# Regrouping TensorE's small-tile products in a planned attention, mixture-of-experts and channel-mix kernel

## The chip, the cores and the metric

The kernel runs on one core of one Trainium2 chip. The metric is the device time of one execution in microseconds (us). Three runs of the kernel before took 386.15, 383.17 and 384.91 us; the median is 384.91 us.

## The reference, cut to what matters

Three stages follow each other, all in float32. Two sequences of 768 tokens are processed.

```python
# stage 1: 8 heads of 64, a local window of 16 plus 24 block summaries
k_sum = k.reshape(B, H, nb, block, D).max(axis=3)
v_sum = v.reshape(B, H, nb, block, D).mean(axis=3)
scores_all = concat([where(|i - j| < 16, q @ k.T / 8, -1e9), q @ k_sum.T / 8 + log(32)])
x = softmax(scores_all) @ concat([v, v_sum])
...
# stage 2: 4 experts, each a causal attention of its own (Hd = 64); the best 2 per token are summed
for e in range(E):
    a = softmax(causal((x @ wq[e]) @ (x @ wk[e]).T / 8))
    ye = a @ (x @ wv[e]) @ wo[e]
    out += (e in topk) * w_e * ye
...
# stage 3: channel mix
k = maximum(xk @ w_k, 0); v = (k * k) @ w_v; r = sigmoid(xr @ w_r); return r * v
```

`xk` and `xr` are mixes of each token with the one before it.

## The kernel before, in words

Stage 1 goes over 12 tiles of 128 tokens (six per sequence). For a tile, `stage1_scores` makes the scores of 4 head pairs (L585: products of 64 rows by 64 columns, a quarter of TensorE's array each); VectorE (DVE) adds the mask and takes the maximum (L599), ScalarE (ACT) the exponential (L602), the rows are normalized (L610, on GpSimd (POOL), DVE or ACT); `stage1_trans` turns the weights with TensorE (PE, L637: full array) into PSUM, and ACT or DVE copies them out (L368, L369); `stage1_out` multiplies them with the values (L655: half of the array per product), and ACT and DVE copy the result from the one bank "a1" into `x` as a high and a low part (L368, L376). The means of the values per block (`val_sums0`, L516) are products with a matrix of ones kept in `cst`; they need all value tiles of the first sequence, and ACT, DVE and POOL then copy them into 12 value tiles (`put_val_sums`, L368, L369, L371) before a tile's L655.

Stage 2 goes over 4 chunks of 384 tokens: projections (`proj_all`, L734, L771), scores of each expert (L846, L847; DVE L855, ACT L865), and for each pair of experts `attend`: the weights are cut into 128x128 blocks, three blocks make a block group, each group is turned for both experts (L906: full array), evicted by ACT or DVE into a buffer `th`, and multiplied with the values into the bank "a2" (L926: half of the array per product). A chunk of the first half of a sequence has 2 groups per expert pair, one of the second half 5. L937 multiplies the sum with the gate, L960 is the output projection.

Stage 3: `rec` (L1068), `hid` (L1090) and `vout` (L1113) per chunk, all on the full array. Its weights are converted by DVE and ACT first (L1003 to L1012).

Nothing runs in the order in which it is written. Every piece is recorded as an operation with a cost; `Plan.run` then places operations one at a time on the engine that is free first, by its own clock and by priorities (`BIAS` per stream), and the program is emitted in that order. Each engine works strictly in the emitted order. For PE the planner adds `tail` (47 to 52 ns) when the next operation is of another stream. A recorded operation is never interrupted by another one, but between two operations the planner may put anything. Before, the scores of a tile are 4 operations, and each run of blocks of L926 one operation, recorded one block group behind the transposes. Six PSUM banks "ps" are shared by all; buffers are given out in turn from numbered slots (`th` 4).

## Time and profile before

| | us |
|---|---|
| median of three runs | 384.91 |
| the profiled execution, its own time | 389.32 |
| span of its instructions in the profile | 387.5 |
| PE busy in the span | 363.2 |
| DVE busy | 274.3 |
| ACT busy | 230.4 |
| POOL busy | 78.9 |
| stage 3's last part on PE, from the first L1113 on | 145.4 |

How to read it: the profiled execution took 389.32 us as a whole; the profile's rows count from its first instruction and reach over 387.5 us, so 1.8 us lie around them. A row of a timeline gives start, duration, engine, line and the tiles; rows of one kind that follow each other are merged (x16), and in brackets stands how long the engine stood still before and what ended it. PE's matrix products are pipelined: the duration of a row reaches past the start of the next, so the price of a product is read from start to start. Float32 products are recorded once per pass, so a row's count is that of passes. Granted clock 1.00 is 2.4 GHz, 0.50 is 1.2 GHz.

### The profile page before, as it was taken

What the parts mean: (1) busy time and instruction counts of PE and PEld (TensorE: products, weight loads), DVE (VectorE), ACT (ScalarE), POOL (GpSimd) and SP (SyncE); (2) the same over time, 40 slices, a digit from 0 to 9 for tenths busy, and PEclk for the clock granted to TensorE, in tenths of its full rate; (3) what the DMA queues carried; (4) which work ended last, traced back from release to release, by engine and by line L of the source; (5) the groups of instructions that cost most, each with busy time, mean ns of one, the idle gap of its engine ahead of it and who ended that gap; (6) DMA issues with size and microseconds to landing.
All of it is one profiled execution on the core that took longest, in us unless ns stands there. A gap on an engine that the chain in (4) does not pass through costs nothing.

```text
span 387.5 us, 7433 instructions
## 1 busy us (share of the span) xinstructions
PE 363.2 (94%) x2704; PEld 304.9 (79%) x2704; DVE 274.3 (71%) x828; ACT 230.4 (59%) x631; POOL 78.9 (20%) x116
## 2 busy tenths in 40 slices
PE   1785999899999999999999999999999999999996
PEld 0554789767768789897787699888988899889986
DVE  2869699899999899797999999913870196202511
ACT  2967786989877886688678976404550256014500
POOL 5204601344431201150353143200010001000000
PEclk9997699999999999999999999999999999999999
DMA  8993445846041142100131530010001000100001
GB/s 273 234 287 113 137 151 162 209 146 188 26 151 57 28 143 62 43 2 0 56 108 44 176 108 2 27 54 2 0 2 54 27 3 0 47 36 1 2 27 54
DMA packets 18596, 31.41 MB, mean 81 GB/s; under 512 B 1792, under 2 KB 8960, under 8 KB 18560
## 3 DMA queue, kind: packets, MB, share of 16 engines
q1 hardware_dynamic: 18560, 30.94, 26.3%
q8 instruction: 21, 0.34, 0.4%
q14 instruction: 15, 0.12, 0.1%
HBM read 27.79 MB, written 3.15 MB: 80 GB/s over the span
## 4 chain that ended last, share of the span: by engine, by line
PE 81%; DVE 9%; DMA 7%; ACT 2%; issue 1%; SPq 0%; DVEq 0%; ACTq 0%
PE ps L1090 18%; PE ps L1113 17%; PE ps L1068 9%; PE ps L734 6%; PE a L926 5%; PE ps L960 4%; PE ps L771 4%; PE ps L906 4%; PE ps L585 3%; PE a L655 3%; PE ps L846 3%; PE ps L637 2%; PE ps L847 2%; DMA vw<-in_vp 2%; DMA qb<-in_qT 2%; DMA stage<-in_vp 2%
## 5 line engine op out<-in xcount | busy, mean ns | idle before, releaser
L602 ACT ACTIVATE pp<-pp,nm 128x120 f32<-128x120 f32 x96 | 36.7, 384 | 7.6 <-DVE nm L599 7.3
L865 ACT ACTIVATE pq<-pq,nm 128x128 f32<-128x128 f32 (+5 forms) x48 | 31.8, 664 | 8.8 <-DVE nm L855 7.0
L1119 DVE TENSOR_TENSOR wvgl<-ps,pp 128x512 f32<-128x512 f32 (+1 forms) x13 | 8.5, 650 | 39.2 <-PE ps L1113 39.2
L368 ACT ACTIVATE pp<-ps 128x512 f32<-128x512 f32 x11 | 6.6, 597 | 49.4 <-PE ps L1068 49.4
L734 PE MATMUL ps<-x,wqkh 128*128 128x384 f32 x128 | 35.1, 355 | 0.0
L855 DVE CUSTOM_DVE_ANT_0 pq<-ps,trm 128x384 f32<-128x384 f32 (+3 forms) x64 | 30.8, 500 | 1.0 <-PE ps L847 0.5
L1096 DVE SCALAR_TENSOR_TENSOR q<-ps,q 128x384 f32<-128x384 f32 x32 | 17.5, 553 | 17.3 <-ACT q L1095 17.0
L906 PE MATMUL ps<-cst,pq 128*128 128x128 f32 x168 | 28.3, 276 | 0.1
L585 PE MATMUL ps<-kw,qb 64*64 64x120 f32 x320 | 15.6, 314 | 11.2 <-DMA qb<-in_qT 7.8
L1006 POOL TENSOR_SCALAR f<-f 128x512 f32<-128x512 f32 x11 | 17.3, 1573 | 41.0 <-ACT f L1003 31.9
L637 PE MATMUL ps<-cst,pp 128*120 128x128 f32 x96 | 19.4, 319 | 5.7 <-DVE pp L610 4.0
L599 DVE CUSTOM_DVE_ANT_0 pp<-ps,msk 128x120 f32<-128x120 f32 x96 | 21.8, 274 | 4.0 <-PE ps L585 3.9
L926 PE MATMUL a<-th,vv 128*64 128x384 f32 (+2 forms) x144 | 24.4, 435 | 0.3 <-DVE fs L937 0.3
L376 DVE TENSOR_TENSOR x<-q,x 128x384 fp32r<-128x384 f32 x23 | 12.9, 581 | 16.3 <-ACT x L368 16.1
L1095 ACT ACTIVATE q<-ps 128x384 f32<-128x384 f32 x32 | 15.7, 489 | 14.1 <-PE ps L1090 12.8
L846 PE MATMUL ps<-ks,q 128*128 128x384 f32 (+3 forms) x64 | 22.2, 352 | 1.2 <-DVE nm L855 0.6
L637 PEld LDWEIGHTS ps<-cst,pp 128*120 128x120 f32 x96 | 12.3, 154 | 13.8 <-issue 9.6
L906 PEld LDWEIGHTS ps<-cst,pq 128*128 128x128 f32 x168 | 20.2, 140 | 3.6 <-issue 0.7
L368 ACT ACTIVATE th<-ps 128x384 f32<-128x384 f32 x46 | 21.2, 487 | 2.8 <-PE ps L906 2.5
L734 PEld LDWEIGHTS ps<-x,wqkh 128*128 128x128 f32 x128 | 21.2, 189 | 1.8 <-issue 1.0
L585 PEld LDWEIGHTS ps<-kw,qb 64*64 64x64 f32 x320 | 10.3, 156 | 15.3 <-ACT kw L368 11.2
L771 PE MATMUL ps<-wvgh,x 128*128 128x260 f32 x96 | 21.9, 292 | 0.0
(231 smaller groups left out, 1050.5 us busy)
## 6 DMA issues: line engine op xcount, KB each, us to landing
stage<-in_wk SPq DMA_DIRECT2D x8, 512.0 KB, 3.5
stage<-in_wv SPq DMA_DIRECT2D x8, 512.0 KB, 3.6
qb<-in_qT SPq DMA_DIRECT2D x12, 256.0 KB, 5.3
vw<-in_vp SPq DMA_DIRECT2D x16, 192.0 KB, 3.3
out_y<-wvgl SPq DMA_DIRECT2D x11, 256.0 KB, 2.0
stage<-in_wr SPq DMA_DIRECT2D x4, 512.0 KB, 3.8
kw<-in_kS SPq DMA_DIRECT2D x6, 320.0 KB, 3.8
ks<-in_kS SPq DMA_DIRECT2D x4, 400.0 KB, 5.2
```

Source lines behind the costliest of these rows:

```text
L585: mm(ps[par].t[c, i * NK:(i + 1) * NK], q.t[r, i, c], k.t[r, i, o:o + NK], start=True, stop=True)
L602: op("act", act(NK, True) + 186, lambda i=i: nc.scalar.activation(pr.t[:, i], pr.t[:, i], AF.Exp, bias=nm.t[:, i:i + 1], scale=-1.0, accum ...
L637: lambda i=i: nc.tensor.transpose(p.t[:NK, i * P:(i + 1) * P], pr.t[:, i], ident()),
L734: mm(p.t[:, :C], a.t[:, kc, cols], x.t[:, kc, :], start=(kc == 0 and i == 0), stop=(kc == KC - 1 and i == 2))
L771: mm(p.t[:, :260], x.t[:, kc, tok], a.t[:, kc, :], start=(kc == 0 and i == 0), stop=(kc == KC - 1 and i == 2))
L846: mm(p.t[:, :z - a], q1.t[:, e, tok], ks.t[:, e, a:z], start=True, stop=False)
L865: op("act", act(nk, True) + 186, lambda pr=pr, nm=nm, nk=nk, i=e2 * TPC + tq, m=nc_: nc.scalar.activation(pr.t[:, :nk], pr.t[:, :nk], AF.E ...
L906: lambda i=i, kb=kb, pr=pr: nc.tensor.transpose(p.t[:, i * P:(i + 1) * P], pr.t[:, kb * P:(kb + 1) * P], ident()),
L926: mm(acc.t[64 * e2:64 * e2 + 64, tq0 * P:(tq0 + cnt) * P], vv.t[:, kb, e * D:(e + 1) * D], ths[e2].t[:, i0 * P:(i0 + cnt) * P], start=firs ...
L1068: mm(p.t, a.t[:, kc, tok], w[2](), start=(kc == 0 and i == 0), stop=(kc == KC - 1 and i == 2))
L1090: mm(p.t[:, :C], w[2]()[:, mo:mo + P], a.t[:, kc, :], start=(kc == 0 and i == 0), stop=(kc == KC - 1 and i == 2))
L1113: mm(p.t[:, :n], a[2]()[:, tok], w[2]()[:, col], start=(m == 0 and i == 0), stop=(m == FC - 1 and i == 2))
```

## The change

PE's array can be cut: a product of 64 by 64 uses a quarter ("quarter"), one of 128 rows by 64 columns a half ("half"), the rest the whole ("full"). The change names this mode for each PE operation and regroups the operations:

- the planner charges 150 or 190 ns whenever the next PE operation has another mode (it was 47 to 52 ns for another stream), and the costs of the small products are lowered accordingly;
- the four score operations of a tile of stage 1 become one (two for the first tile);
- the value products of `attend` are recorded in steps: both groups in one operation for a chunk of 2 groups, groups 0 and 1 and then 2, 3 and 4 for a chunk of 5; the transposes of the next group are recorded ahead of a step;
- `th` gets 6 slots instead of 4, `ksm` 1 instead of 2, and the matrix of ones moves from `cst` into a tile `own` of its own that uses a slot of `x2` (one more transfer of 368 bytes per partition; `cst` has 672 instead of 1040).

```diff
-SLOTS = dict(th=4, pt=3, pp=4, stage=2)
+SLOTS = dict(th=6, pt=3, pp=4, stage=2)
...
+    SWITCH = {(a, b): 150.0 if a == "full" else 190.0 for a in ("full", "half", "quarter") for b in (
+        "full", "half", "quarter") if a != b}
...
-                if last_pe is not None and last_pe.stream != o.stream:
-                    t = max(t, clock["pe"] + last_pe.tail)
+                if last_pe is not None and last_pe.mode != o.mode:
+                    t = max(t, clock["pe"] + self.SWITCH[last_pe.mode, o.mode])
...
-    cst = buf("cst", [P, P + 5 * NB - 4 + 16])
+    cst = buf("cst", [P, P + NB + 16])
+    own = buf("x2", [P, 4 * NB - 4])
...
-                op("pe", 300, go, r=[cst, (v, "win")] + ([(v, "sum")] if s2 == 0 else []), w=[p], stream="p1v",
-                   tail=52.0)
+                op("pe", 230, go, r=[own, (v, "win")] + ([(v, "sum")] if s2 == 0 else []), w=[p], stream="p1v",
+                   mode="quarter")
...
-                def go(i=i, ps=ps):
+            def go(lo=lo, hi=hi, ps=ps):
+                for i in range(lo, hi):
                     for s2 in range(2):
...
-                op("pe", 260, go, r=[q] + kr, w=[(p, i) for p in ps], stream="p1", claim=prs + nms, tail=52.0)
+            op("pe", 205 * (hi - lo), go, r=[q] + kr, w=[(p, i) for p in ps for i in range(lo, hi)], stream="p1",
+               claim=prs + nms, mode="quarter")
...
-            several("p1o", GROUP["p1o"], i, 4, 331, av, r=[pts[0][0], pts[1][0], vs[0], vs[1]],
-                    w=[(p, i)], tail=52.0)
+            several("p1o", GROUP["p1o"], i, 4, 234, av, r=[pts[0][0], pts[1][0], vs[0], vs[1]],
+                    w=[(p, i)], mode="half")
...
-                    op("pe", pe_f(cnt * P, 64) + 60, go, r=ths + [(vv, kb)], w=[acc], stream="p2a", tail=47.0)
-
-            prev = None
-            for gi in range(len(groups) + 1):
-                cur = [tr(gi, e2) for e2 in range(2)] if gi < len(groups) else None
-                if gi > 0:
-                    vmm(gi - 1, prev)
-                prev = cur
...
+                op("pe", sum(18.0 + 1.9 * r[6] * P for r in runs), go,
+                   r=sum((ths[gi] for gi in some), []) + [(vv, r[4]) for r in runs], w=[acc], stream="p2a", mode="half")
...
+            steps = ((0, 1), (2, 3, 4)) if len(groups) == 5 else ((0, 1),)
+            for i, some in enumerate(steps):
+                ahead = some[-1] + (i + 1 < len(steps))
+                for gi in range(len(ths), ahead + 1):
+                    ths[gi] = [tr(gi, e2) for e2 in range(2)]
+                vmm(some)
```

Since the planner's costs change, the whole order changes. Counted over PE's instructions, the mode changes 112 times in the order before and 58 times in the changed one; from the first projection (the first L734) on, 92 and 41 times, 35 of the 92 in the stretch of 86 to 126 us of the profile. The same products stand ahead of the first projection in both orders: the scores of six tiles, the value sums, 36 transposes of stage 1 and the value products of four tiles. Value products of `attend` are visited 28 times before and 12 times now, scores of stage 1 22 and 10 times.

Three places show it. The first is PE in the second chunk's `attend` (`a_316` and `a_317` are the bank of the sum, `th` the turned block groups, `pq` the weights, `pp` weights of stage 1). Before:

```order
L926 MATMUL a_316_1666<-th_1585,vv_648 64x384
L926 MATMUL a_316_1666<-th_1612,vv_648 64x384
L637 MATMUL ps_1674<-cst_84,pp_1417 120x128 x2
L906 MATMUL ps_1679<-cst_84,pq_292_1234 128x128
L906 MATMUL ps_1679<-cst_84,pq_295_1373 128x128
L906 MATMUL ps_1679<-cst_84,pq_299_1408 128x128
L906 MATMUL ps_1685<-cst_84,pq_303_1480 128x128
L906 MATMUL ps_1685<-cst_84,pq_306_1499 128x128
L906 MATMUL ps_1685<-cst_84,pq_310_1532 128x128
L926 MATMUL a_316_1666<-th_1649,vv_648 64x384
L926 MATMUL a_316_1666<-th_1658,vv_648 64x384
```

And now:

```order
L913 MATMUL ps_1616<-cst_84,pq_307_1424 128x128
L913 MATMUL ps_1616<-cst_84,pq_311_1436 128x128
L939 MATMUL a_317_1625<-th_1553,vv_640 64x384
L939 MATMUL a_317_1625<-th_1564,vv_640 64x384
L939 MATMUL a_317_1625<-th_1579,vv_640 64x384
L939 MATMUL a_317_1625<-th_1592,vv_640 64x384
L662 MATMUL a_277_1639<-pt_1539,vw_113 64x64
L662 MATMUL a_277_1639<-pt_1546,vw_113 64x64
```

Two block groups now stand together, and stage 1's value products (also half) follow them without a change of mode.

The second is PE at the scores of stage 1's sixth tile, shortly ahead of the first projection (`ps_584`, `ps_585` and `ps_583`, `ps_584` are the banks of the scores, `pp_430` and `pp_458` the weights of the tile before). Before:

```order
L637 MATMUL ps_579<-cst_84,pp_430 120x128
L585 MATMUL ps_584<-kw_144,qb_90 64x120
L585 MATMUL ps_585<-kw_144,qb_90 64x120
...
L637 MATMUL ps_579<-cst_84,pp_430 120x128
...
L655 MATMUL a_95_619<-pt_488,pq_26_74 64x64
```

And now:

```order
L644 MATMUL ps_575<-cst_84,pp_458 120x128 x4
L591 MATMUL ps_583<-kw_146,qb_94 64x120
L591 MATMUL ps_584<-kw_146,qb_94 64x120
...
L662 MATMUL a_96_613<-pt_516,pq_27_74 64x64
```

Before, two of the four transposes stand between score operations; now all four stand ahead of them.

The third is DVE where the value sums (`vs`) have become ready and are copied into the value tiles (`pp` are weights of stage 1, the ISA rows their masks). Before:

```order
L610 TENSOR_TENSOR pp_286<-pp_286,rss_217 128x480
L369 COPY vw_67<-vs_409 24x512
L369 COPY vw_105<-vs_409 24x512
L369 COPY vw_122<-vs_409 24x512
L369 COPY oh_70<-vs_409 24x512
L369 COPY ol_135<-vs_409 24x512
L605 TENSOR_REDUCE rss_217<-sms_63 128x4
```

And now:

```order
L373 COPY vw_67<-vs_370 24x512
L617 TENSOR_TENSOR pp_302<-pp_302,rss_221 128x480
L606 ISA pp_374,nm_376<-ps_372,msk_76 128x120
...
L606 ISA pp_375,nm_377<-ps_373,msk_76 128x120
...
L373 COPY oh_70<-vs_370 24x512
```

Two of the twelve copies are left on DVE and stand apart; ACT has three (one before) and POOL seven (six before).

## Rows read from the trace of the kernel before

**Rows 1.** The page's shares of the chain of work that ended last, by engine.

```profile
PE 81%; DVE 9%; DMA 7%; ACT 2%; issue 1%; SPq 0%; DVEq 0%; ACTq 0%
```

**Rows 2.** Busy time by stretch: start and end in us, length, busy us (instructions) of PE, of PE's weight loads, DVE, ACT and POOL, the granted clock, DMA share, GB/s. The first stretch is from the first L734 to the first L1113, the second from there to the end.

```profile
46.30:242.08 195.78, 192.00 (x1549) 157.98 (x1546) 181.43 (x574) 155.84 (x429) 57.02 (x76) 1.00 0.31 94
242.08:387.50 145.42, 142.44 (x709) 125.54 (x707) 62.20 (x120) 44.79 (x88) 5.74 (x6) 1.00 0.06 22
```

**Rows 3.** PE's timeline ahead of the first projection.

```profile
34.81 1.08 PE L637 MATMUL ps<-cst,pp 128*120 128x128 f32 x4 [2.86 <-DVE pp L610]
35.83 1.98 PE L655 MATMUL a<-q,vw 120*64 120x64 f32 x32
39.23 0.48 PE L655 MATMUL a<-pt,oh 120*64 120x64 f32 x4 [1.42 <-DVE x L376]
...
41.13 1.54 PE L637 MATMUL ps<-cst,pp 128*120 128x128 f32 x6
...
45.24 1.15 PE L655 MATMUL a<-pt,pq 120*64 120x64 f32 x32
46.32 0.62 PE L734 MATMUL ps<-x,wqkh 128*128 128x384 f32 x2
```

**Rows 4.** Busy time by stretch, as in rows 2, for the two microseconds in which the granted clock changes.

```profile
34.00:35.00 1.00, 0.19 (x1) 0.22 (x2) 1.00 (x4) 1.00 (x5) 0.17 (x1) 0.67 0.82 193
44.00:45.00 1.00, 1.00 (x14) 0.57 (x17) 0.02 (x1) 0.01 (x1) 0.00 (x0) 0.71 0.75 263
```

**Rows 5.** Busy time by stretch, as in rows 2, for the 40 us in which stage 1 and stage 2 run side by side.

```profile
86.00:96.00 10.00, 10.00 (x163) 8.17 (x159) 9.97 (x48) 10.00 (x39) 3.87 (x7) 1.00 0.60 186
96.00:106.00 10.00, 10.00 (x86) 7.82 (x88) 9.73 (x44) 8.85 (x28) 4.70 (x5) 1.00 0.15 39
106.00:116.00 10.00, 9.71 (x98) 6.33 (x94) 9.78 (x22) 7.43 (x19) 3.79 (x3) 1.00 0.48 147
116.00:126.00 10.00, 9.95 (x75) 8.09 (x76) 9.72 (x52) 6.87 (x21) 1.45 (x3) 1.00 0.15 55
```

**Rows 6.** PE's timeline around value products of the last chunk that stand among products of `rec`.

```profile
199.46 0.86 PE L1068 MATMUL ps<-kw,x 128*128 128x512 f32 x3
200.16 0.86 PE L1068 MATMUL ps<-vw,x 128*128 128x512 f32 x3
...
201.48 0.87 PE L926 MATMUL a<-th,vv 128*64 128x384 f32 x4
202.28 0.96 PE L1068 MATMUL ps<-vw,x 128*128 128x512 f32 x3
203.16 0.65 PE L926 MATMUL a<-th,vv 128*64 128x256 f32 x4
```

**Rows 7.** The chain of work that ended last, in order of time (start, us, what): two block groups in one visit.

```profile
177.27 1.45 PE a L926 x12
```

**Rows 8.** PE's timeline around value products of the second chunk that stand among transposes.

```profile
132.14 0.87 PE L926 MATMUL a<-th,vv 128*64 128x384 f32 x4
132.94 0.43 PE L637 MATMUL ps<-cst,pp 128*120 128x128 f32 x2
133.21 0.82 PE L906 MATMUL ps<-cst,pq 128*128 128x128 f32 x6
133.96 0.87 PE L926 MATMUL a<-th,vv 128*64 128x384 f32 x4
```

**Rows 9.** PE's timeline at scores of stage 1: two tiles' scores in one visit, and a tile's scores cut by single transposes.

```profile
67.08 1.87 PE L585 MATMUL ps<-kw,qb 64*64 64x120 f32 x64
68.89 0.44 PE L906 MATMUL ps<-cst,pq 128*128 128x128 f32 x2
...
86.96 0.82 PE L637 MATMUL ps<-cst,pp 128*120 128x128 f32 x6
...
88.28 0.32 PE L637 MATMUL ps<-cst,pp 128*120 128x128 f32 x1
88.53 0.44 PE L585 MATMUL ps<-kw,qb 64*64 64x120 f32 x8
88.90 0.33 PE L637 MATMUL ps<-cst,pp 128*120 128x128 f32 x1
...
89.52 1.15 PE L655 MATMUL a<-pt,vw 120*64 120x64 f32 x32
```

**Rows 10.** DVE's timeline: the first mask row of the third tile's scores, and the copies of the value sums.

```profile
23.82 0.28 DVE L599 CUSTOM_DVE_ANT_0 pp<-ps,msk 128x120 f32<-128x120 f32 x1 [3.02 <-PE ps L585]
...
29.11 2.38 DVE L369 COPY vw<-vs 24x512 f32<-24x512 f32 x3 [0.38 <-ACT vs L368]
31.50 0.74 DVE L369 COPY oh<-vs 24x512 f32<-24x512 f32 x1
32.25 0.74 DVE L369 COPY ol<-vs 24x512 f32<-24x512 f32 x1
```

**Rows 11.** PE's timeline: the third tile's scores, which a transpose cuts in two.

```profile
20.64 1.08 PE L585 MATMUL ps<-f,qb 64*64 64x120 f32 x16 [0.96 <-DMA qb<-in_qT]
...
22.69 1.08 PE L585 MATMUL ps<-f,qb 64*64 64x120 f32 x16
```

**Rows 12.** The transfer queue's timeline: the issue of `cst`.

```profile
3.53 0.43 SPq L359 DMA_DIRECT2D cst<-in_consts  x1
```

**Rows 13.** Instructions that write `th`: count, then ns min/median/max.

```profile
L368 ACT ACTIVATE th<-ps x46: 471/489/509, 82.4 to 219.5; 128x384 f32<-128x384 f32 x46
```

More of the change, by code (lines that the diff above doesn't have):

```diff
@@ L76 @@
     __slots__ = ("ways", "eng", "cost", "fn", "preds", "succs", "bufs", "prio", "start", "end", "need", "seq", "late",
-                 "est", "prev", "stream", "tail", "lock")
+                 "est", "prev", "stream", "mode", "lock")
 class Plan:
@@ L109, in buf, with op @@
         return b
-    def op(self, eng, cost, fn, r=(), w=(), stream=None, late=0.0, bias=0.0, claim=(), ways=(), tail=0.0, lock=False):
+    def op(self, eng, cost, fn, r=(), w=(), stream=None, late=0.0, bias=0.0, claim=(), ways=(), mode="full", lock=False):
         o = Op()
@@ L115, in op @@
         o.eng, o.cost, o.fn, o.seq, o.late = eng, cost, fn, len(self.ops), late
-        o.prev, o.stream, o.tail = None, stream, tail
+        o.prev, o.stream, o.mode = None, stream, mode
         if stream:
@@ L329, in attn_moe_rwkv @@
     consts: bass.AP,
+    owns: bass.AP,
     out: bass.AP,
@@ L395, in attn_moe_rwkv, with several @@
     held = {}
-    def several(stream, size, i, n, cost, fn, r, w, claim=(), tail=0.0):
+    def several(stream, size, i, n, cost, fn, r, w, claim=(), mode="full"):
         g = held.setdefault(stream, [])
@@ L408, in several @@
             op("pe", sum(o[0] for o in ops), go, r=sum((o[2] for o in ops), []), w=sum((o[3] for o in ops), []),
-               stream=stream, claim=claim, tail=tail)
-    cst = buf("cst", [P, P + 5 * NB - 4 + 16])
+               stream=stream, claim=claim, mode=mode)
+    cst = buf("cst", [P, P + NB + 16])
+    own = buf("x2", [P, 4 * NB - 4])
     msk = buf("msk", [P, 3, NK])
@@ L918, in vmm, with one @@
                         runs.append([kb, i, 1, tq])
-                for ri, (kb, i0, cnt, tq0) in enumerate(runs):
+                return [(gi, ri, len(runs), ths, *x) for ri, x in enumerate(runs)]
+            def vmm(some):
+                fns = []
+                runs = sum((runs_of(gi, ths[gi]) for gi in some), [])
+                for gi, ri, n, th, kb, i0, cnt, tq0 in runs:
                     first = gi == 0 and ri == 0
-                    last = gi == len(groups) - 1 and ri == len(runs) - 1
-                    def go(kb=kb, i0=i0, cnt=cnt, tq0=tq0, first=first, last=last):
+                    last = gi == len(groups) - 1 and ri == n - 1
+                    def one(th=th, kb=kb, i0=i0, cnt=cnt, tq0=tq0, first=first, last=last):
                         for e2 in range(2):
@@ L926, in go @@
                             mm(acc.t[64 * e2:64 * e2 + 64, tq0 * P:(tq0 + cnt) * P], vv.t[:, kb, e * D:(e + 1) * D],
-                               ths[e2].t[:, i0 * P:(i0 + cnt) * P], start=first, stop=last)
-                    op("pe", pe_f(cnt * P, 64) + 60, go, r=ths + [(vv, kb)], w=[acc], stream="p2a", tail=47.0)
-            prev = None
-            for gi in range(len(groups) + 1):
-                cur = [tr(gi, e2) for e2 in range(2)] if gi < len(groups) else None
-                if gi > 0:
-                    vmm(gi - 1, prev)
-                prev = cur
+                               th[e2].t[:, i0 * P:(i0 + cnt) * P], start=first, stop=last)
+                    fns.append(one)
+                def go():
+                    for fn in fns:
+                        fn()
+                op("pe", sum(18.0 + 1.9 * r[6] * P for r in runs), go,
+                   r=sum((ths[gi] for gi in some), []) + [(vv, r[4]) for r in runs], w=[acc], stream="p2a", mode="half")
+            ths = {}
+            steps = ((0, 1), (2, 3, 4)) if len(groups) == 5 else ((0, 1),)
[4 more added lines that the diff above has]
+                vmm(some)
             op("dve", dve(C), lambda: nc.vector.tensor_tensor(f.t, acc.t[:, :C], f.t, ALU.mult), r=[acc], w=[f])
@@ L1135, in attn_moe_rwkv @@
             load(lambda: msk.t[:, 0], masks[:, 0], P * NK * 4, 480, w=[(msk, 0)])
-    load(lambda: cst.t, consts, P * 1040, w=[cst])
+    load(lambda: cst.t, consts, P * 672, w=[cst])
+    load(lambda: own.t, owns, P * 368, w=[own])
     load_q(1)
```

17 lines of the change are left out of this document (9 added, 8 removed).

## The prediction

> **What bounds the kernel now.** I read the chain of work that ended last first: PE holds 81% of it [rows 1]. Then the busy times by stretch. From the first projection (46.3 us) to the first product of `vout` (242.08) PE is busy 192.00 of 195.78 us, and from there to the end nothing but PE's full-array products runs, 145.42 us of them [rows 2]. The change leaves these last products as they are, so that part stays. Two things can move: when the first projection starts, and how long PE takes from there to `vout`. The same products stand ahead of the first projection in both orders, so this start is a mark that can be compared.
>
> Ahead of the mark PE's timeline [rows 3] shows waits: PE stands still 2.86 us before the transposes at 34.81 and 1.42 us before the value products at 39.23. Behind the first of these the granted clock falls: from 34 to 35 us its mean is 0.67, and only from 44 to 45 us does it rise again [rows 4]; in between it is 0.50. So the same 32 passes of L655 take 1.98 us at 35.83 and 1.15 us at 45.24 [rows 3].
>
> Behind the mark PE is full, but DVE nearly is too: 181.43 of 195.78 us [rows 2], and 39.20 of the 40 us from 86 to 126 [rows 5]. That is the number that speaks most against the change, and it comes back below.
>
> **The change, part 1: fewer changes of mode.** What does one cost? Among products of `rec` [rows 6], a visit of three L1068 products takes 0.70 us from start to start (199.46 to 200.16); behind a visit of L926, and with the next one following, it takes 0.88 (202.28 to 203.16), 0.18 more. The L926 visit itself takes 0.80 (201.48 to 202.28) for one block group. Two groups in one visit take 1.45 [rows 7], so a group alone is 0.65 and the visit adds 0.15. In and out together cost 0.33 us. Among transposes [rows 8] the period is 1.82 us (132.14 to 133.96): a group of 0.65, eight transposes at 0.11 (six span 0.82 with the last one's 0.27 us tail, so five pitches in 0.55), and 0.29 left. For the scores [rows 9]: 64 passes, eight operations, take 1.81 us in one visit (67.08 to 68.89); one operation with a transpose between takes 0.62 (88.28 to 88.90). With about 0.21 per operation and 0.11 for the transpose, 0.30 is left. The three prices lie at 0.29 to 0.33; I take 0.31 per pair, 0.155 per change. Behind the mark the changes fall from 92 to 41. 51 x 0.155 = **7.9 us** of PE time, all in a stretch where PE stands still only 3.78 of 195.78 us [rows 2].
>
> Does PE keep it? 35 of the 92 lie between 86 and 126 us, where DVE has 0.8 us of 40 left [rows 5]. Their share of the saving is 35/92 x 7.9 = 3.0; if DVE cannot be packed closer than there at its best (9.97 of 10), 0.7 of it remains. In the rest of the stretch DVE is busy 142.2 of 155.8 us and has 13.6 us to give, more than the 4.9 that are asked. So 7.9 - 3.0 + 0.7 = 5.6 is what DVE leaves, 7.9 what PE could have. Part of DVE's time in these 40 us belongs to weights of stage 3 that aren't yet asked for and may slide, so I take **6.5**, between the two. The lowest end: the new order makes PE stand still for 3.8 us more, as much again as now, on top of DVE's bound: 1.8.
>
> **Part 2: the order ahead of the first projection.** Four things change there, and one costs.
> - Value sums. DVE copies five of them in a row, 29.11 to 32.99, 3.86 us [rows 10], with the masks of the fourth tile behind them in the queue; PE waits for a normalized tile from DVE until 34.81 [rows 3]. Now two copies stand on DVE, apart. The three that leave are 3 x 0.77 = 2.3 us. ACT and POOL take them, and value products wait for these copies as well, so I count half: 1.15 (ends 0 and 2.3).
> - Scores as one operation. The third tile's second half starts at 22.69, behind a transpose; it could follow the first at 20.64 + 1.08 = 21.72 [rows 11]. DVE, which stood still 3.02 us for it until 23.82 [rows 10], starts **1.0** earlier.
> - The clock. If PE doesn't stand still for 2.86 us, the clock need not fall. It costs 0.83 at the second tile's value products (1.98 against 1.15), 0.82 at the third's (39.23 to 41.13 against 45.24 to 46.32), and 1.55 in the run of transposes and scores that follows (41.13 to 45.24 is 4.11; the same run at full clock, 86.96 to 89.52, is 2.56) [rows 3, 9]: **3.2** together. In the changed order a transpose and the fifth tile's scores stand between the first two tiles' value products, and what these wait for is an ACT and a DVE copy out of the bank. I count on standstills of about 1.4 us, the one that stands before 39.23 now, and on the clock holding. Ends 0 and 3.2.
> - Three mode changes fewer here: 3 x 0.155 = **0.5**.
> - The transfer for `own`. A transfer takes 0.43 us to issue [rows 12], and those behind it move back by at most two of these if the queue is the limit, or by nothing if the bytes are. I take **0.3** lost.
>
> Together 1.15 + 1.0 + 3.2 + 0.5 - 0.3 = **5.5 us**; the first L734 then starts at about 40.8. Ends: 1.2 with no copy won and the clock falling, 6.7 with all of it.
>
> **What costs nothing.** `th` with 6 slots, `ksm` with one and `own` in a slot of `x2` delay nothing that I can find: `x2` is first written by the output projection L960 of the first chunk, behind a whole chunk's attention, and the value sums are done ahead of the first projection. If `own` held its slot longer, it would be L960's eviction that waits. The counts of DVE, ACT and POOL instructions stay the same to within a few. Grouped visits come later than single ones; what is late next would be L937 and the bank of the sum, and PE has projections or output products between in the order.
>
> **The sum.** 5.5 + 6.5 = 12.0. Against the profiled execution: 389.32 - 12.0 = 377.3. The runs' median is 4.4 below that execution, so 384.91 - 12.0 = **372.9 us**.
>
> **The rivals.**
> - *DVE sets the pace.* For it: 39.20 of 40 us [rows 5]. Against it: 14.35 us of DVE's time are free over the whole stretch [rows 2]. Then the late gain is 0.7 in those 40 us and half of the other 4.9, 3.1 in all: 384.9 - 5.5 - 3.1 = 376.3. The Trainium skill, page "TensorEngine Tiling (Array Packing)", section "PSUM Bottleneck", speaks for this case: tiling makes TensorE faster but not the emptying of PSUM, which can become the bottleneck. By that rule the sum would be 376.3, by the free time in the rows 372.9; the rows at 86 to 126 us are on the rule's side, those of the other 156 us are not.
> - *The clock falls all the same.* For it: standstills stay in the early part, since the bank "a1" must be emptied between two tiles' value products. Against it: 2.86 us was the one ahead of the fall. Early gain 5.5 - 3.2 = 2.3: 384.9 - 2.3 - 6.5 = 376.1. With DVE setting the pace too: 384.9 - 2.3 - 3.1 = 379.5.
> - *Visits wait for evictions* (the other side). A visit of two or three groups needs four or six evicted buffers at once, and PE's whole queue stands behind it. Before, the next group's six transposes covered an eviction of 0.49 us [rows 13]. If each of the 12 visits waits for two evictions in turn on ACT, 0.98 us, the 12 us are gone (384.6); at three, 1.47 us, it is 12 x 1.47 - 12.0 = 5.6 slower, 390.5. It decides from 1.0 us per visit. Against it: other products stand between transposes and visit nearly everywhere in the order.
> - *Mode changes are hidden behind waits anyway.* Then the late gain would be near nothing and 379.4 would stand, the same time as the two rivals together; PE's standstill of 3.78 us in the stretch speaks against it.
>
> **How the numbers follow.** Forecast 0.48; DVE's pace 0.17; the clock 0.17; both, or hidden changes, 0.10; evictions 0.08. The measurement tells about 1% from no change: 381.1 and 388.8. Forecast, DVE and clock end below 381.1: 0.82; of the next case half does (0.05), half falls short (0.05). Of the evictions 0.05 is slower, 0.03 about even. So faster 0.87, same 0.08, slower 0.05. The range reaches up to 380.5, just over the two rivals together, and down to 368.5, where both parts give all that their ends allow (6.7 + 7.9 = 14.6, 370.3) and half of PE's 3.78 us goes too. The forecast's own range is 370 to 376.
>
> **What would show it.** First L734 at 40 to 42 us and no stretch of 0.50 behind 30 us (part 2); if the clock falls there, that step is wrong. From the first L734 to the first product of `vout` about 189 us instead of 195.8, with DVE at 0.95 or more (part 1); PE's busy share there is no measure, since changes of mode hide in it. Idle of PE's weight loads or of PE ahead of L939, put down to ACT or DVE, would show the evictions; DVE at 0.99 from 80 to 120 us with PE waiting for masks would show the first rival. The last part must stay at 145.4 us.

## The result, and the profile after

| | before | after |
|---|---|---|
| median, us (runs) | 384.86 (4) | 374.74 (4) |
| lowest and highest, us | 383.17, 386.15 | 374.16, 375.44 |
| ratio after to before | | 0.9709, 95% interval 0.9661 to 0.9756 |
| the profiled execution, us | 389.32 | 374.65 |
| span in the profile, us | 387.5 | 372.9 |

The change makes the kernel 2.9% faster by the ratio on record; the two medians lie 10.1 us apart, which is 2.6%, inside the ratio's interval. The profiled spans differ by 14.6 us; where the other 4.5 come from is part of what follows. One profiled execution of an experiment (e4_after_relief) took 843.67 us against 372.66 to 373.87 for its other runs; its rows aren't used.

First the page's shares of the chain of work that ended last, after the change:

```profile
PE 57%; DVE 20%; ACT 10%; DMA 7%; issue 3%; POOL 1%; SPq 1%; POOLq 0%; DVEq 0%
```

Before, PE had 81% [rows 1]. In the part between the first projection and stage 3's last products the chain now changes between engines.

Busy time by stretch (columns as in rows 2). The windows of [rows 2] miss the marks a little: the first L1113 starts at 241.92, not 242.08. From mark to mark, before:

```profile
46.32:241.92 195.60, 191.81 (x1548) 157.82 (x1545) 181.25 (x574) 155.82 (x429) 56.84 (x76) 1.00 0.31 94
241.92:387.53 145.61, 142.60 (x709) 125.70 (x708) 62.37 (x120) 44.79 (x88) 5.90 (x6) 1.00 0.06 22
```

And after; the third and fourth line answer to [rows 4], the rest to [rows 5]:

```profile
36.23:227.66 191.43, 185.50 (x1549) 159.12 (x1546) 179.73 (x583) 156.32 (x435) 57.44 (x75) 1.00 0.33 99
227.66:372.88 145.22, 142.08 (x709) 125.48 (x708) 61.39 (x119) 45.78 (x90) 4.68 (x5) 1.00 0.06 22
...
34.00:35.00 1.00, 1.00 (x35) 0.82 (x32) 1.00 (x5) 1.00 (x4) 0.00 (x0) 1.00 0.02 6
44.00:45.00 1.00, 1.00 (x10) 0.75 (x11) 0.76 (x2) 0.98 (x3) 1.00 (x2) 1.00 0.00 0
...
86.00:96.00 10.00, 9.78 (x118) 8.06 (x119) 9.96 (x53) 9.88 (x38) 2.50 (x3) 1.00 0.26 72
96.00:106.00 10.00, 9.70 (x93) 8.04 (x92) 9.20 (x30) 8.40 (x25) 4.93 (x5) 1.00 0.46 146
106.00:116.00 10.00, 10.00 (x128) 8.49 (x127) 9.81 (x51) 9.93 (x34) 3.21 (x8) 1.00 0.18 55
116.00:126.00 10.00, 9.91 (x82) 7.27 (x82) 9.02 (x16) 7.65 (x18) 2.53 (x2) 1.00 0.37 117
```

The stretch from the first projection (now L741) to the first product of `vout` (now L1135) went from 195.60 to 191.43 us, 4.2 less. PE's busy time in it fell by 6.3 (191.81 to 185.50), and its standstills grew from 3.8 to 5.9. Four more profiles of experiments with the changed order up to the first product of `vout` (e1_tail_full, e1_tail_half, e5_after_warm, e5_after_warm2) have 190.6 to 191.9 us there, two more of the order before (e3_before_again, e3_before_warm) 195.7 and 196.1, so the gain there lies between 3.7 and 5.5 us. The last part is 145.22, 0.4 less than before. The granted clock reads 1.00 everywhere. DVE has 37.99 busy us of the 40 from 86 to 126, before 39.20.

PE's timeline of the kernel after, ahead of the first projection (answers to [rows 3, 11]):

```profile
11.70 2.80 PE L591 MATMUL ps<-kw,qb 64*64 64x120 f32 x48 [3.21 <-ACT kw L372]
...
19.02 1.05 PE L591 MATMUL ps<-f,qb 64*64 64x120 f32 x32
...
28.66 1.15 PE L662 MATMUL a<-q,vw 120*64 120x64 f32 x32 [0.54 <-DVE x L380]
...
31.45 0.34 PE L662 MATMUL a<-pt,oh 120*64 120x64 f32 x4 [1.05 <-DVE x L380]
...
32.96 1.27 PE L644 MATMUL ps<-cst,pp 128*120 128x128 f32 x8 [0.36 <-POOL pp L617]
34.17 1.05 PE L591 MATMUL ps<-kw,qb 64*64 64x120 f32 x32
35.15 1.15 PE L662 MATMUL a<-pt,pq 120*64 120x64 f32 x32
36.23 0.45 PE L741 MATMUL ps<-x,wqkh 128*128 128x384 f32 x1
```

The first projection comes at 36.23 instead of 46.32 us. The third tile's scores are one piece of 1.05 us at 19.02. Between 20 us and the first projection the longest standstill is 1.05; the 2.86 us of before is gone. The copies of the value sums on DVE (answers to [rows 10]) have become two single ones:

```profile
24.51 0.39 DVE L373 COPY vw<-vs 24x512 f32<-24x512 f32 x1
26.20 0.61 DVE L373 COPY oh<-vs 24x512 f32<-24x512 f32 x1
```

Grouped visits in the chain that ended last (answers to [rows 7]): two groups take 1.45 us as before, three 2.09, so the third adds 0.64.

```profile
165.93 1.45 PE a L939 x12
...
186.66 2.09 PE a L939 x16
```

What PE waited for from 36.2 to 227.5 us after the change (us in total, times, longest):

```profile
PE ps L853 <- DVE ks L380: 1.7, 3, 1.2
PE ps L546 <- PE ps L741: 0.7, 1, 0.7
PE ps L546 <- POOL stage L542: 0.7, 1, 0.7
```

None of them is a visit (L939): the evictions of `th` don't hold the grouped visits up.

### The profile page after: what moved, and what is told of

It is laid out like the page before. It is cut to its first block, busy times and chain, and to the rows that moved or that the text cites. A ratio compares the mean times of both kernels' runs of the same rounds, so it can differ in the third digit from the quotient of the medians.

```text
span 372.9 us, 7436 instructions
## 1 busy us (share of the span) xinstructions
PE 350.1 (94%) x2704; PEld 301.9 (81%) x2704; DVE 268.5 (72%) x831; ACT 229.0 (61%) x631; POOL 78.0 (21%) x113
## 4 chain that ended last, share of the span: by engine, by line
PE 57%; DVE 20%; ACT 10%; DMA 7%; issue 3%; POOL 1%; SPq 1%; POOLq 0%; DVEq 0%
PE ps L1112 18%; PE ps L1135 18%; PE ps L1090 9%; ACT pp L609 4%; DVE pq L862 3%; PE ps L982 3%; DMA stage<-in_vp 2%; PE a L939 2%; DVE ks L380 2%; DMA qb<-in_qT 2%; PE ps L913 2%; DMA ol<-in_vp 2%; PE ps L741 2%; DMA ks<-in_kS 2%; DVE ql L380 1%
## 5 line engine op out<-in xcount | busy, mean ns | idle before, releaser
L741 PE MATMUL ps<-x,wqkh 128*128 128x384 f32 x128 | 35.1, 355 | 0.4 <-DVE nm L862 0.4
L380 DVE TENSOR_TENSOR x<-q,x 128x384 fp32r<-128x384 f32 x25 | 13.7, 559 | 16.3 <-ACT x L372 16.1
L853 PE MATMUL ps<-ks,q 128*128 128x384 f32 (+3 forms) x64 | 22.4, 353 | 2.8 <-DVE ks L380 1.7
L741 PEld LDWEIGHTS ps<-x,wqkh 128*128 128x128 f32 x128 | 21.5, 189 | 1.4 <-DVE nm L862 0.6
L591 PE MATMUL ps<-kw,qb 64*64 64x120 f32 x320 | 12.2, 297 | 10.5 <-ACT kw L372 10.5
L741 PE MATMUL ps<-x,wqkl 128*128 128x384 f32 x64 | 21.6, 338 | 0.0
L1112 PE MATMUL ps<-x,wqkh 128*128 128x384 f32 x96 | 21.4, 335 | 0.0
L939 PE MATMUL a<-th,vv 128*64 128x384 f32 (+2 forms) x144 | 20.8, 423 | 0.1
L854 PE MATMUL ps<-ks,ql 128*128 128x384 f32 (+3 forms) x64 | 20.3, 322 | 0.0
L1073 DVE SCALAR_TENSOR_TENSOR q<-x,mu,q 128x384 f32<-128x384 f32 x32 | 19.0, 608 | 1.0 <-ACT q L391 1.0
```

What stands on the lines that cost most here:

```text
L380: ways = [("dve", dve(n), lambda: nc.vector.tensor_tensor(dst(), a(), b().bitcast(F32), ALU.subtract), sb)]
L741: mm(p.t[:, :C], a.t[:, kc, cols], x.t[:, kc, :], start=(kc == 0 and i == 0), stop=(kc == KC - 1 and i == 2))
L853: mm(p.t[:, :z - a], q1.t[:, e, tok], ks.t[:, e, a:z], start=True, stop=False)
L939: mm(acc.t[64 * e2:64 * e2 + 64, tq0 * P:(tq0 + cnt) * P], vv.t[:, kb, e * D:(e + 1) * D], th[e2].t[:, i0 * P:(i0 + cnt) * P], start=first ...
L1112: mm(p.t[:, :C], w[2]()[:, mo:mo + P], a.t[:, kc, :], start=(kc == 0 and i == 0), stop=(kc == KC - 1 and i == 2))
```

## The experiments

Theory 1: a pair of mode changes costs 0.31 us of PE, and the fewer changes behind the first projection are the late gain. Theory 2: the order ahead of the first projection, with the clock that no longer falls, is the early gain. Rivals: the price isn't one of modes; DVE sets the pace; the new schedule alone, or chance of the profiled run, is the gain.

### The price of a mode change

```diff
                         mm(p.t[:, :n], a[2]()[:, tok], w[2]()[:, col], start=(m == 0 and i == 0),
                            stop=(m == FC - 1 and i == 2))
+                    mm(extra.t[:, 0:64], cst.t[:, 0:P], cst.t[:, 0:64], start=True, stop=True)
```

That is e1_tail_full; in e1_tail_half the added line is

```diff
+                    mm(extra.t[0:64, 0:64], cst.t[:, 0:64], cst.t[:, 0:64], start=True, stop=True)
```

> The changed kernel, with one small product of 128 x 128 by 64 columns put behind each of the 104 groups of three products of the last stage (vout), into a bank that nothing reads. It keeps the array in full mode, so both theories expect the same: 104 times the bare cost of the small product, which I put at 0.07 to 0.15 us, so 7 to 16 us more than 374.7. It is the base for the next run.

> The same small products, but with 64 stationary columns, so that each is a visit in half mode: 104 pairs of mode changes more, in a stretch where PE does nothing but products and is busy 142.2 of 145.4 us. Theory 1 (a pair of mode changes costs 0.31 us of PE's time) expects 104 x 0.31 = 32 us above the kernel with the full small products. Rival (the 0.29 to 0.33 us read from the trace came from what stood around those visits, such as a bank's hand-over, not from the mode): the same time as that kernel, within 3 us.

Measured: 397.17 us with the full products, 422.58 with the half ones (medians of 2 runs each). The difference is 25.4 us for 104 pairs: **0.244 us per pair, 0.122 per change** (0.233 per pair between the faster runs of each, 0.255 between the slower). The rival (same time) falls. The price is one of mode, but 0.31 was a quarter too high. It is measured for changes between full and half; changes to and from quarter were not measured by themselves. PE's timeline of e1_tail_half shows one such visit (two passes) between products of `vout`:

```profile
249.66 0.97 PE L1135 MATMUL ps<-vv,pq 128*128 128x512 f32 x3
250.56 0.33 PE L1137 MATMUL a<-cst 128*64 128x64 f32 x2
250.82 0.51 PE L1135 MATMUL ps<-vv,pq 128*128 128x512 f32 x1
251.16 0.40 PE L1135 MATMUL ps<-woh,pq 128*128 128x512 f32 x1
251.40 0.39 PE L1135 MATMUL ps<-vv,pq 128*128 128x512 f32 x1
```

The product behind the visit takes 0.34 us to the start of the next, an undisturbed one 0.24 (251.16 to 251.40). The full products themselves cost 0.216 us each (397.17 - 374.74 over 104), more than the 0.07 to 0.15 expected.

### The clock ahead of the first projection

The kernel before, unchanged, for its profile:

> The kernel before once more, for its profile. If the fall of the granted clock at 34 us is a thing of some runs only, this profile may show none: clock 1.00, first projection near 43 us and a profiled time of 384 to 386, the median of its runs. If every run has it, the profile shows 0.987 again, first projection at 46.3, and the profiled execution is some 4 us above the median for another reason. Both expect 1.00 as the ratio.

Its ratio is 0.9986 (0.9952 to 1.0020), and the truth lies between the two expectations. PE's timeline, and below it busy time by stretch:

```profile
19.01 0.64 PE L585 MATMUL ps<-f,qb 64*64 64x120 f32 x16 [1.52 <-DMA qb<-in_qT]
...
31.79 0.74 PE L637 MATMUL ps<-cst,pp 128*120 128x128 f32 x4 [2.85 <-DVE pp L610]
32.50 1.98 PE L655 MATMUL a<-q,vw 120*64 120x64 f32 x32
...
42.06 0.62 PE L734 MATMUL ps<-x,wqkh 128*128 128x384 f32 x2
```

```profile
32.00:39.00 7.00, 5.58 (x74) 4.88 (x72) 6.47 (x29) 6.34 (x26) 1.25 (x1) 0.51 0.34 107
```

The same standstill of 2.85 us, and the clock falls behind it, for 7 us instead of 10. But the first projection comes at 42.06, not 46.32: here the third tile's 16 passes took 0.64 us at 19.01, in the first profile 1.08 [rows 11]. PE had left the half pace of its start by then (the last section has more on it). So 4.3 us of the profiled difference are no doing of the change: the transposes behind the standstill start 3.0 us later in the first profile (34.81 against 31.79), a slow start of that one execution, and from there to the first projection it takes 1.2 us longer (11.51 against 10.27), the longer fall of the clock.

Of these 10 runs none had a mean clock above 0.991, but the fall isn't in every run. Among the 52 runs of the kernel before that were timed beside the experiments and lie within 1.5% of the fastest, 4 have a mean clock of 1.000 and a median of 383.23 us, 21 have 0.991 (385.19) and 15 have 0.987 (386.45). So the fall costs 2.0 us in the commonest case and 3.2 in the next, and where the clock of the kernel before holds, it still takes some 8.5 us more than the changed kernel.

The standstill filled, in the kernel before:

```diff
                             mm(ps[par].t[c, i * NK:(i + 1) * NK], q.t[r, i, c], k.t[r, i, o:o + NK],
                                start=True, stop=True)
+                    if (t, i) == (4, 3):
+                        for _ in range(32):
+                            mm(spare["p"].t[:, 256:320], cst.t[:, 0:P], cst.t[:, 0:64], start=True, stop=True)
```

> The kernel before, in the same order, with 32 small full-array products behind the fifth tile's scores, into a bank that nothing reads any more, so that PE doesn't stand still at 32.0 to 34.8 us. Theory 2 (the fall of the granted clock to 0.50 follows that standstill and costs 3.2 us ahead of the first projection): no stretch at 0.50 behind 30 us, first projection at 43 us instead of 46.3 in the profile, and a median 3 us (0.8%) below the kernel before if the clock falls in every one of its runs. If the fall is a thing of some runs only, the profile shows the same but the medians differ by under 1 us. Rival (the fall doesn't hang on the standstill): the clock falls here too, first projection at 46, ratio 1.00.

Ratio 1.0003 (0.9975 to 1.0031), clock 1.000. I had mis-sized the filling; PE's timeline:

```profile
29.22 7.36 PE L589 MATMUL a<-cst 128*128 128x64 f32 x64
36.42 0.60 PE L640 MATMUL ps<-cst,pp 128*120 128x128 f32 x4
...
44.30 0.62 PE L737 MATMUL ps<-x,wqkh 128*128 128x384 f32 x2
```

The small products took 7.2 us, more than the 2.8 of the standstill, and delayed the transposes to 36.42. From there to the first projection it is 7.88 us, against 10.27 in e3_before_again (31.79 to 42.06) and 11.51 in the first profile [rows 3]. So in these 12 runs, where PE had work, the clock didn't fall (0.999 to 1.000), and its fall costs 2.4 us (7 us of it) to 3.6 (10 us), near the 2.0 and 3.2 of the runs above. The run shows the price; as a gain it is cancelled by the delay of 4.6 us.

The slow start, in the changed kernel, with small products ahead of the first scores:

```diff
+    def warm():
+        z = wo_l.t[:, 0].bitcast(F32)
+        mm(spare["p"].t[:, 0:64], z[:, 0:P], z[:, 0:64], start=True, stop=True)
...
             def go(lo=lo, hi=hi, ps=ps, cold=cold):
+                for _ in range(28 if cold else 0):
+                    warm()
                 for i in range(lo, hi):
...
+                for _ in range(14 if cold else 0):
+                    warm()
```

> The changed kernel, in the same order, with 28 small full-array products ahead of the first scores and 14 behind their first half, into a bank that nothing reads. In the changed kernel the first 64 passes of the scores run at about half the pace of later ones (48 passes in 2.80 us at 11.70) although the granted clock reads 1.00. If that pace comes from PE having done nothing before, the 48 passes take 1.4 to 1.6 us here and the value-sum products behind them 1.3 instead of 1.9; the first projection comes 0.5 to 1.5 us before 36.2, and the median is 0.5 to 1.5 us below 374.7. If the pace comes from something else (late operands), it stays at 2.8 us, and the median within 0.5 us of 374.7.

383.60 us, 9 above the changed kernel. PE's timeline:

```profile
1.44 12.21 PE L564 MATMUL a<-wol 128*128 128x64 f32 x56 [1.44 <-DVE wol L1204]
13.57 1.08 PE L599 MATMUL ps<-kw,qb 64*64 64x120 f32 x16
14.58 6.23 PE L564 MATMUL a<-wol 128*128 128x64 f32 x28
20.75 2.58 PE L599 MATMUL ps<-kw,qb 64*64 64x120 f32 x48
```

Again the filling was too long (0.22 us a pass). And 18 us of it did not end the half pace: the 48 passes still took 2.58 us. So the reason as I had put it (PE had done nothing before) was wrong. The same with wide products, 11 and 7 of 512 columns:

```diff
-        z = wo_l.t[:, 0].bitcast(F32)
-        mm(spare["p"].t[:, 0:64], z[:, 0:P], z[:, 0:64], start=True, stop=True)
+        z = wo_l.t[:, 0]
+        mm(spare["p"].t, z[:, 0:P], z, start=True, stop=True)
```

> The changed kernel, in the same order, with 11 full-array products of 512 columns ahead of the first scores and 7 behind their first half (in place of the small ones of the run before, which took 0.44 us each and so delayed everything by 9 us, and after which the scores still ran at half pace). If the half pace of the start ends after wide products, the 48 passes of the scores take 1.4 to 1.6 us instead of 2.8, the first projection comes up to 1.5 us before 36.0, and the median falls below 374.7 by 0.5 to 1.5. If it ends only some time after the start whatever PE does, they take 2.8 us, and the products ahead of the scores, at 0.47 us each, cost nothing or up to 1 us.

```profile
1.44 4.78 PE L564 MATMUL a<-wol 128*128 128x512 f32 x11 [1.44 <-DVE wol L1204]
7.04 0.76 PE L599 MATMUL ps<-kw,qb 64*64 64x120 f32 x16 [0.82 <-ACT kw L372]
7.73 1.88 PE L564 MATMUL a<-wol 128*128 128x512 f32 x7
11.01 1.58 PE L599 MATMUL ps<-kw,qb 64*64 64x120 f32 x48 [1.40 <-ACT kw L372]
```

Now the 48 passes take 1.58 us. The first projection comes at 35.57, half a microsecond earlier, but the time is 374.45 (ratio 0.9700, 0.9656 to 0.9745): no measurable gain over the change. Behind the scores PE then waited for two value tiles (0.30 and 0.43 us) and a sum on DVE (0.45), and the stretch behind the mark took 191.85 us.

### Merges and schedule apart

Four kernels: the new schedule with neither merge, with one, and both merges under the old schedule rule.

One block group per visit (e2_groups1, e2_planner_only):

```diff
-            steps = ((0, 1), (2, 3, 4)) if len(groups) == 5 else ((0, 1),)
+            steps = tuple((g,) for g in range(len(groups)))
```

One score operation per pair of heads (e2_scores1, e2_planner_only):

```diff
-            op("pe", 205 * (hi - lo), go, r=[q] + kr, w=[(p, i) for p in ps for i in range(lo, hi)], stream="p1",
-               claim=prs + nms, mode="quarter")
+                op("pe", 205, go, r=[q] + kr, w=[(p, i) for p in ps], stream="p1", claim=prs + nms, mode="quarter")
```

The old rule, with the old costs (e6_merges):

```diff
-                if last_pe is not None and last_pe.mode != o.mode:
-                    t = max(t, clock["pe"] + self.SWITCH[last_pe.mode, o.mode])
+                if last_pe is not None and last_pe.stream != o.stream:
+                    t = max(t, clock["pe"] + self.TAIL.get(last_pe.stream, 0.0))
```

> The changed kernel with both merges undone: value products of one block group per visit and scores as one operation for each pair of heads, but the schedule still counts mode changes. Behind the first projection it changes mode 90 times (before 92, changed kernel 41), ahead of it 26 times (20 and 17). Theory 1 (fewer mode changes give the late gain): from the first projection to the first product of vout 194 to 196 us, as before. Rival (the planner's new costs and slots give it): 191 to 192. Theory 2 (ahead of the first projection it is the scores as one operation that count): first projection at 39 to 42 us, time 381 to 384. Rival (the copies of the value sums moved off DVE by the new plan count): 36 to 38 us.

> The changed kernel with only the grouped visits undone: one block group per visit. 77 mode changes behind the first projection instead of 41, and the same order ahead of it. Theory 1: 36 more changes, at the rate that was kept (4.5 us for 51) 3.2 us, at the full price 5.6 us, so 378 to 380.3; first projection at 36.2 as in the changed kernel. Rival (DVE sets the pace, changes are hidden behind waits): within 1.5 us of 374.7.

> The changed kernel with only the scores of stage 1 put back to one operation for each pair of heads. 65 mode changes behind the first projection instead of 41, 26 ahead of it instead of 17. Theory 1: 24 more changes behind, 2.1 to 3.7 us. Theory 2 (the early gain comes from scores in one piece): first projection 3 to 6 us later than 36.2, so 380 to 384 in all. Rival (the early gain comes from the value-sum copies and the plan): first projection at 36 to 38, 377 to 379 in all.

> The changed kernel with both merges, but a schedule made by the old rule and the old costs (a fixed tail where the stream of products changes, no count of mode changes). It changes mode 47 times behind the first projection (changed kernel 41, before 92) and 15 times ahead of it (17, 20). If the merges carry the gain under either schedule: 190 to 193 us from the first projection to the first product of vout, first projection at 35 to 38, ratio to before 0.965 to 0.978. If the counting of mode changes by the schedule is what makes the merges pay: 194 us or more there, ratio 0.985 or more.

| kernel | ratio to before (95%) | changes behind, ahead of the mark | first projection | stretch | PE busy in it | standing still |
|---|---|---|---|---|---|---|
| before, two profiles | 1 | 92, 20 | 46.32, 42.06 | 195.6, 195.7 | 191.8, 191.6 | 3.8, 4.1 |
| e6_merges | 1.0018 (0.9980 to 1.0057) | 47, 15 | 42.81 | 195.9 | 188.8 | 7.0 |
| e2_planner_only | 1.0163 (1.0120 to 1.0207) | 90, 26 | 39.42 | 204.5 | 194.4 | 10.1 |
| e2_scores1 (groups merged) | 0.9964 (0.9931 to 0.9996) | 65, 26 | 39.14 | 197.3 | 190.4 | 6.9 |
| e2_groups1 (scores merged) | 0.9884 (0.9845 to 0.9924) | 77, 17 | 36.05 | 197.2 | 191.3 | 5.8 |
| after | 0.9709 (0.9661 to 0.9756) | 41, 17 | 36.23 | 191.4 | 185.5 | 5.9 |

All times in us from the profiles; the mark is the first projection. All four kernels keep the new slots and the tile `own`, and each is one order that the planner made; another order with the same counts was not tried. The lines behind the experiments' rows, busy time by stretch, first of e6_merges:

```profile
42.80:238.65 195.85, 188.84 (x1548) 161.23 (x1545) 180.04 (x575) 158.35 (x436) 53.07 (x70) 0.98 0.31 94
...
66.00:76.00 10.00, 7.53 (x59) 5.72 (x59) 8.22 (x51) 8.72 (x41) 3.99 (x7) 0.66 0.74 200
```

of e2_planner_only:

```profile
39.40:243.88 204.48, 194.43 (x1543) 158.80 (x1542) 182.34 (x584) 157.55 (x433) 55.69 (x72) 0.99 0.30 93
...
70.00:80.00 10.00, 6.65 (x57) 5.18 (x53) 7.88 (x39) 7.01 (x31) 1.47 (x5) 0.83 0.65 177
```

of e2_scores1:

```profile
39.14:236.50 197.36, 190.43 (x1543) 160.06 (x1542) 181.65 (x592) 156.96 (x431) 48.84 (x69) 0.98 0.32 96
```

and of e2_groups1:

```profile
36.05:233.20 197.15, 191.34 (x1548) 158.59 (x1545) 183.49 (x588) 157.51 (x439) 53.33 (x66) 1.00 0.31 96
```

Neither half of the change is a gain by itself. **The schedule alone makes the kernel 1.6% slower, the merges alone change nothing, and both together give 2.9%.** What theory 1 expected of single merges held in direction, and the sizes came out larger: e2_groups1, with 36 more changes, has 5.7 us more in the stretch and 5.9 more in PE's busy time (0.16 per change); its whole is 6.7 us over the changed kernel by the ratios (384.86 x 0.0175), over the 3.2 to 5.6 expected. e2_scores1 has 5.9 us more in the stretch for 24 changes, over the 2.1 to 3.7 expected, with the clock at 0.50 for part of it. Theory 2 held for both kernels with cut scores: first projection at 39.14 and 39.42, 383.62 us for e2_scores1; but e2_planner_only took 392.82, not 381 to 384. And scores in one piece are not enough: e6_merges has them and its first projection comes at 42.81. What theory 1 expected of e2_planner_only (194 to 196 us with 90 changes) failed by 8.5: PE stands still 10.1 us there, 2 of them in one piece at 72 to 74, and the clock falls. e6_merges was to show whether the merges carry the gain under either schedule, and they don't: PE is busy 2.7 to 3.0 us less than before, and stands still as much longer. From 66 to 76 us PE is busy 7.5 of 10 there and the mean clock is 0.66, a fall that the changed kernel doesn't have; what the merges alone would give in the stretch without it is not shown.

Ahead of the mark e6_merges shows what the new schedule is for. DVE's timeline, then PE's:

```profile
25.74 2.38 DVE L373 COPY vw<-vs 24x512 f32<-24x512 f32 x3 [0.38 <-ACT vs L372]
28.13 0.73 DVE L373 COPY oh<-vs 24x512 f32<-24x512 f32 x1
28.88 0.74 DVE L373 COPY ol<-vs 24x512 f32<-24x512 f32 x1
```

```profile
31.20 1.06 PE L644 MATMUL ps<-cst,pp 128*120 128x128 f32 x4 [3.20 <-DVE pp L617]
32.92 1.97 PE L662 MATMUL a<-q,vw 120*64 120x64 f32 x32 [0.67 <-DVE x L380]
```

The five copies stand in a row on DVE again as in [rows 10], from 25.74 to 29.62. Behind them DVE normalizes the tile that PE waits for (L617 from 30.39, 0.66 us). PE stands still 3.20 us, the clock falls at 31.2 for 10 us, and the same 32 passes take 1.97 us as at the fallen clock of [rows 3].

### DVE out of the way

```diff
-        op("dve", dve(512), lambda: nc.vector.scalar_tensor_tensor(
-            g(), raw.t[:, :, 1], SIGN, g(), ALU.bitwise_and, ALU.bitwise_or), r=[raw], w=[(fg, 1)], lock=True)
-        op("dve", dve(512), lambda: nc.vector.scalar_tensor_tensor(
-            f(), f(), 3, g(), ALU.logical_shift_left, ALU.bitwise_or), r=[(fg, 1)], w=[(fg, 0)], lock=True)
+        op("dve", dve(512), lambda: None,
+           r=[raw], w=[(fg, 1)], lock=True)
+        op("dve", dve(512), lambda: None,
+           r=[(fg, 1)], w=[(fg, 0)], lock=True)
```

> The changed kernel in the same order, without two of the operations on DVE that put the bits of each stage-3 weight together (it leaves these out, so the outputs differ); DVE loses some 27 us of its 180 in the stretch from the first projection to the first product of vout. If DVE's bound took back part of what PE was spared (PE busy fell by 6.6 us there and its standstills grew from 3.8 to 5.1 to 5.9), the stretch falls from 190.6 to 191.4 to 188 to 189, with PE standing still 3 us or less. If the standstills come from elsewhere (order, POOL, transfers), it stays at 190.5 to 191.4.

> The kernel before with the same two operations left out, in its own order. Its stretch from the first projection to the first product of vout was 195.7 us with 3.8 us of PE's standstills. If PE was the bound there, 195 or more; if DVE held it as much as it holds the changed kernel, 193 to 194. The difference to the run above is what the change is worth behind the first projection with DVE out of the way: 6.6 us or more if DVE took back part of the gain, 4.5 to 5 if not.

Busy time by stretch of e4_before_relief:

```profile
41.50:236.12 194.62, 191.40 (x1548) 157.73 (x1545) 159.78 (x537) 155.86 (x429) 56.45 (x78) 1.00 0.31 95
```

DVE's 21 us less (180.81 in e3_before_again) shorten the stretch by 1.1, to between the two times expected. The medians are 383.63 and 373.02 (the second of three runs, without the one of 843.67), ratios 0.9941 (0.9904 to 0.9977) and 0.9671 (0.9611 to 0.9731). With DVE relieved the change is worth 10.6 us, without 10.1. The stretch of e4_after_relief wasn't seen; its median is 1.7 us under the changed kernel's, within the intervals. So nothing shows DVE's load taking the missing part of the late gain. That it takes none is not shown: the interval of the second ratio alone is 2.3 us wide to either side.

## Why the prediction came out as it did

The forecast was 372.9 us, the time is 374.74, within its range and its likeliest case. The direction, the place of the gains (ahead of the mark and behind it, next to nothing in the last part) and, within 2 us, the sum of 12.0 against 10.1 were right. The terms were not. That the sum came so near is in part luck: the late gain and the clock were put too high, the scores too low.

- **What bounds the kernel.** Right for the last part (145.22 after 145.61) and for PE behind the mark. The 4.4 us between the profiled execution and the median were carried along unexplained. The second profile of the same code took 4.15 us less (385.17 against 389.32), 3.0 of them by its faster start and 1.2 by the shorter fall of the clock.
- **Part 1, price.** 0.31 us per pair was too high: 0.244 measured in the last part, where nothing else moves. 51 changes at 0.122 are 6.2 us, and PE's busy time fell by 6.3, not 7.9.
- **Part 1, what PE keeps.** 6.5 predicted, 4.2 measured (3.7 to 5.5 over all profiles). The step that failed is "5.6 is what DVE leaves", with DVE as the only thing that takes a share: relieving DVE of 21 us brought 1.1 us of the stretch in the kernel before, and in the 40 full microseconds DVE even has more room than before. What is lost are 2.1 us more of standstills, which the prediction had only in its lowest end, and they wait for single results, the keys' low parts (L853 on `ks`, 1.7 of 5.9 us) first. Whether another order would remove them was not tried.
- **Part 2, size.** 5.5 predicted. Between executions whose starts differ little it is 42.06 - 36.05 = 6.0; the 10.1 of the two profiles hold 4.3 of the slow start and the longer fall. Of its parts the clock is 2.0 to 2.4 where 3.2 was predicted, read from a fall of 10 us that the commonest runs don't have. Scores cut as in e2_scores1, with 9 changes of mode, cost 3.1 (39.14 - 36.05), where 1.0 for the third tile and 0.5 for mode changes stood: I had priced the cut of the third tile alone, but the order of before cuts the fifth and the sixth too, and in e2_scores1 PE stands still 1.70 and 1.64 us where the changed kernel has 1.05 at most. But the parts can't be added up: e6_merges has the scores in one piece and loses 6.8 us to the changed kernel ahead of the mark (42.81 - 36.05), more than the clock and the copies were priced at. How much of the 6.0 is the merge of the scores and how much the new order around it stays open.
- **Copies, standstill, clock.** In e6_merges the copies in a row, the standstill of 3.20 us behind them and the fallen clock come back together, and in e3_before_warm the clock holds where the standstill is filled. No run moves the copies alone.
- **What the prediction did not see.** It took the new costs of the schedule as mere means to merged visits. They decide: the same merges under the old rule and costs give nothing (1.0018), and the new ones without merges lose 1.6%. The rival "mode changes are hidden anyway" came near to e6_merges' truth: changes of mode that are spared come back as standstills, unless the order moves too.
- **The rivals.** DVE's pace: no sign of it, within the intervals above. The clock falls all the same: no, 1.000 in all four runs of the changed kernel, though two of the six of e5_after_warm2, which keeps its order, have 0.995. Visits wait for evictions: no such wait in the trace.

The Trainium skill, page "TensorEngine Tiling (Array Packing)", section "Key Properties", says that a change of tiling mode drains TensorE; the 0.244 us per pair agree with a cost of the change and give it a size, though no row shows the drain itself. Its section "PSUM Bottleneck", by which the rival was 376.3, isn't borne out here: in the kernel before, 21 us less on DVE brought 1.1, and after the change no wait of a visit for an eviction stands in the trace.

## What to carry to other kernels

Measure the price of a mode change by itself, in a stretch where nothing else moves, before multiplying it by a count; here it was 0.12 us a change. Merging operations and telling the planner what they cost belonged together here: either one alone moved work into standstills. And profile the kernel before twice: where two executions of the same code differ by 4 us ahead of a mark, the difference of two traces is no measure of a change.

## What had not been expected of the hardware

At the start of an execution PE runs at half pace, and the view of the granted clock doesn't show it. 48 passes of scores took 2.80 us at 11.70 in the kernel after, 32 passes 1.05 at 19.02. In the kernel before the half pace lasted past 22.69 us in one execution [rows 11] and had ended by 19.01 in another. The view reads 1.00 there only because it counts time without a record as 1.00: the trace's clock records begin at 24.11 and 15.09 us in these two executions and at 16.54 in the kernel after, each with 1.00, and at these times the products pass to full pace. That the clock was at its lower level before is read from the products; no record says it. So for the start of a kernel the pace has to be taken from the rows of the products.

Behind 84 float32 passes of 64 columns, 18 us of PE's time, 48 passes of scores still took 2.58 us, and the records begin at 23.09; behind 18 products of 512 columns, 6.7 us, the 48 passes took 1.58, and the records begin at 5.77. The Trainium skill, page "TensorE: Matmul & The Clock Gate", section "What's actually happening", says that the lower clock is the state at rest, that activity releases it, and that the moment differs from run to run. The two profiles of the kernel before agree with the last, but they lie 9.0 us apart (15.09 and 24.11), where the page has half a microsecond to either side; here the measurement decides.

The granted clock fell to 0.50, the lower of its two levels, at the end of PE's standstills of 2.86, 2.85 and 3.20 us or within 0.4 us behind them, ahead of the first projection (the kernel before twice, e6_merges), and stayed there for 7 to 10 us. A single standstill of that length isn't needed: the clock also fell at 68.8 us in e6_merges and at 66.0 in e2_scores1, for 6.8 us each, inside standstills of only 1.39 and 1.41 us, after 8 us in which PE had stood still some 2 us in all.
